# Rebalancing attention multiplies over steps 11 to 21, and loading two key blocks ahead of the rest

## The chip, the cores and the metric

One core of one Trainium2 chip. The metric is the device time of one execution in microseconds (us), as the median of several executions. Engines: PE does matrix multiplies and transposes, ACT the exponentials, DVE the copies, casts and small elementwise work, POOL issues most loads and prepares later keys, SP issues the first loads and the stores.

## The reference

Attention with queries pooled in pairs, then a feed-forward part that multiplies two projections.

```python
def _attn_ref(q, k, v):                       # (8, 8, 1152, 64) each
    q_pool = q.reshape(B, H, S // 2, 2, D).mean(axis=3)
    scores = np.matmul(q_pool, k.transpose(0, 1, 3, 2)) / np.sqrt(D)
    attn = np.exp(scores - np.max(scores, axis=-1, keepdims=True))
    attn = attn / (np.sum(attn, axis=-1, keepdims=True) + 1e-09)
    return np.matmul(attn, v)

def _moe_ref(x, w1, w2, w3, w_out):           # x: (4608, 512)
    return ((x @ w1) * (x @ w2) @ w3) @ w_out
```

## The kernel before

The 64 heads are worked on in 32 pairs. The scores of all pairs are one long row of 324 chunks; three chunks make a step, so there are 108 steps. In each step PE computes three chunks of scores into three buffers (`psc`), ACT turns each into exponentials in a ring (`er`), PE multiplies earlier exponentials with v (`attend`, so many per step as the list `PVS` says), and up to two side jobs run: one in a buffer of its own (kind F), one in one of the three score buffers (kind X). Side jobs are the transposes of the next pair's queries and keys, and feed-forward work. A tail of feed-forward work follows.

The first pair's keys and queries are loaded in pieces into the end of the ring:

```python
    q0f = spare(2304, FP32).rearrange("p (t d) -> p t d", d=D)
    k0a = spare(512, FP32).rearrange("p (u j d) -> p u j d", u=2, d=D)
    k0b = spare(1792, FP32).rearrange("p (u j d) -> p u j d", u=2, d=D)
    # ... cut ...
    def load_first():
        src = k[0, 0:2].rearrange("u (p j) d -> p u j d", j=NJ)
        qs = q[0, 0:2].rearrange("u (p t) d -> (u p) t d", t=18)
        nc.sync.dma_start(out=k0a, in_=src[:, :, 0:2, :])
        for c in parts:
            r = slice(2 * c.start, 2 * c.stop)
            nc.sync.dma_start(out=q0f[:, r], in_=qs[:, r])
        nc.sync.dma_start(out=k0b, in_=src[:, :, 2:NJ, :])
    # ... cut: prep_first; stage_keys casts key blocks, move_keys transposes them ...
        spin(25, 128)          # filler multiplies
        stage_keys(0)
        move_keys(0)
        spin(8, 128)
        queries(0)
        spin(5, 128)
        scores(0)
        expo(0)
        queries(1)
        spin(1)
        stage_keys(1)          # casts blocks 2 and 3
        def some():
            move_keys(1)
            stage_keys(2)      # casts blocks 4 to 8
            spin(1)
```

The loads of the pairs after the first are issued in a fixed order, on POOL:

```python
    load_v(0)
    load_q(1)
    load_k(1)
    load_w3(0, 1)
    load_w3(1, 1)
    load_wo(0)
    load_k(2)
    load_q(2)
    load_v(1)
    # ... cut ...
```

The list, and the part of a step that uses it:

```python
    PVS = [
        0, 9, 13, 18, 22, 28, 22, 23, 22, 23, 40, 22, 28, 22, 23, 22, 23, 45,
        45, 18, 18, 18, 18, 18, 45, 18, 27, 45, 45, 18, 18, 18, 26, 18, 27, 21,
        # ... cut ...
    ]
    for it in range(NIT):
        # ... cut: fetch side jobs ...
        for w in range(BURST):
            # ... cut: some(), rest(), the first side jobs ...
            if it or w:
                scores(BURST * it + w)
                expo(BURST * it + w)
        # ... cut: loads, prep_stage (pools queries and casts keys on DVE), prep_groups ...
        n = PVS[it]
        left = 45 - nb % 45
        brief = bool(queue) and queue[0][2] == 1
        a = left if left < n else 8 if brief and it > 8 and 8 < n < 40 and 8 < left < 45 else 0
        pv(a)
        if head():
            group("F")
        if head() and (n < 40 or urgent or it < 17):
            group("X")
        pv(n - a)
        # ... cut ...
```

The softmax here doesn't subtract the row's maximum and nothing guards it: scores larger than these inputs give would overflow.

Of the kernel before, what the change touches and what calls it, by code (L numbers as in the profile page):

```python
# [15 lines left out]
NJ = 9  # L16
# [7 lines left out]
def kernel(  # L24
# [11 lines left out]
    nc = tc.nc  # L36
# [88 lines left out]
    def new_kq(P):  # L125
        if P % 2 == 0:
            kTs[P // 2] = ab.tile([128, 2, NJ, 128], FP16, tag="kT", bufs=2, name="kT")
            qTs[P // 2] = ab.tile([128, NJ, 128], FP16, tag="qT", bufs=2, name="qT")
        o = 64 * (P % 2)
        kT[P] = kTs[P // 2][:, P % 2]  # L130
        qT[P] = qTs[P // 2][:, :, o:o + 64]

    def copy_v(P):
        nc.vector.tensor_copy(out=vts[P % 4][:, :, :, 0:D], in_=vst.pop(P))
# [39 lines left out]
    def spare(n, dt=FP16):  # L174
        nonlocal end
        end -= n
        return er[:, 1, end:end + n].bitcast(dt) if dt != FP16 else er[:, 1, end:end + n]
# [3 lines left out]
    k0b = spare(1792, FP32).rearrange("p (u j d) -> p u j d", u=2, d=D)  # L181
# [4 lines left out]
# [4 lines that stand above are left out]
        for c in parts:  # L190
            r = slice(2 * c.start, 2 * c.stop)
            nc.sync.dma_start(out=q0f[:, r], in_=qs[:, r])  # L192
        nc.sync.dma_start(out=k0b, in_=src[:, :, 2:NJ, :])

    def spin(n, w=512):
        t = psum.tile([128, 512], FP32, tag="ff", bufs=1, name="spin")
        for _ in range(n):
            nc.tensor.matmul(t[:, 0:w], ones[:, 0:128], ones[:, 0:w], start=True, stop=True)

    def prep_first():  # L200

        new_kq(0)
        kc = new_kc(0)
        src = q0f.rearrange("p (c two) d -> p c two d", two=2)
        js = (slice(0, 2), slice(2, 4), slice(4, NJ))

        def stage_keys(n):
            j = js[n]
            copy = nc.vector.tensor_copy if n else nc.scalar.copy
            copy(out=kc[:, j].rearrange("p j u d -> p u j d"),  # L210
                 in_=k0b[:, :, j.start - 2:j.stop - 2] if n else k0a)

        def move_keys(n):
            j = js[n]
            tag = "ff" if n == 2 else "po"
            if n:
                tk = psum.tile([128, 1024], FP16, tag=tag, bufs=1, name="tk")
                keys(0, tk, range(j.start, j.stop))
            else:
                tk = psum.tile([128, 512], FP32, tag=tag, bufs=1, name="tk")  # L220
                for i in range(2):
                    nc.tensor.matmul(tk[:, 128 * i:128 * i + 128],
                                     kc[:, i].rearrange("p u d -> p (u d)"), ident,
                                     start=True, stop=True)
            copy = nc.vector.tensor_copy if n else nc.scalar.copy
            copy(out=kT[0][:, j].rearrange("p j f -> p (j f)"),
                 in_=tk[:, 0:128 * (j.stop - j.start)])

        def queries(h):
            r = parts[h]  # L230
            nc.vector.tensor_tensor(out=q0p[:, r], in0=src[:, r, 0, :], in1=src[:, r, 1, :],
                                    op=ALU.add)
            dt, w = (FP16, 1024) if h else (FP32, 512)
            tq = psum.tile([128, 2, w], dt, tag="psc", bufs=3, name="tq")[:, 0]
            for c in range(r.start, r.stop):
                o = 64 * (c - r.start)
                for u in range(2):
                    x = slice(64 * u, 64 * u + 64)
                    if h:
                        nc.tensor.transpose(tq[x, o:o + 64], q0p[x, c], ident[x, x])  # L240
                    else:
                        nc.tensor.matmul(tq[x, o:o + 64], q0p[x, c], ident[x, x],
                                         start=True, stop=True)
            copy = nc.vector.tensor_copy if h else nc.scalar.copy
            copy(out=qT[0][:, r],
                 in_=tq[:, 0:64 * (r.stop - r.start)].rearrange("p (c f) -> p c f", f=64))

        spin(25, 128)
        stage_keys(0)
        move_keys(0)  # L250
        spin(8, 128)
        queries(0)
        spin(5, 128)
        scores(0)
        expo(0)
        queries(1)
        spin(1)
        stage_keys(1)

        def some():  # L260
            move_keys(1)
            stage_keys(2)
            spin(1)

        def rest():
            move_keys(2)
            copy_v(0)
            del kcs[0]

        return some, rest  # L270
# [168 lines left out]
    def ffn_groups(t):  # L439
# [79 lines left out]
        out=ident, in_=ident, compare_op=ALU.not_equal, fill=1.0,  # L519
# [46 lines left out]
    def head():  # L566
        while not queue and gens:
            g = next(gens[0], None)
            if g is None:
                gens.pop(0)  # L570
            else:
                queue.append(g)
        return bool(queue)
# [35 lines left out]
    for t, c, h in PLAN:  # L609
        early.append((t, w3_group(c) if h is None else T_group(c, h)))  # L610

    PVS = [
        0, 9, 13, 18, 22, 28, 22, 23, 22, 23, 40, 22, 28, 22, 23, 22, 23, 45,
        45, 18, 18, 18, 18, 18, 45, 18, 27, 45, 45, 18, 18, 18, 26, 18, 27, 21,
        34, 35, 18, 27, 18, 27, 25, 30, 45, 45, 18, 18, 18, 18, 18, 45, 18, 27,
        45, 45, 18, 18, 18, 26, 18, 27, 21, 34, 35, 18, 27, 18, 27, 25, 30, 45,
        45, 18, 18, 18, 18, 18, 45, 18, 27, 45, 45, 18, 18, 18, 26, 18, 27, 21,
        34, 35, 18, 27, 18, 27, 25, 30, 45, 45, 18, 18, 18, 18, 18, 45, 45, 18,
    ]
    reached = []  # L620
    next_unit = 0
    for it in range(NIT):
        at = it * BURST * CH / PAIR
        while early and it >= early[0][0]:
            queue.append(early.pop(0)[1])
        while next_unit < EARLY:
            last_b = (512 * (next_unit + 1) - 1) // SQ
            if it < 3 or reached[it - 2] < 360 * (last_b + 1):
                break
            gens.append(ffn_groups(next_unit))  # L630
            next_unit += 1
        for w in range(BURST):
            if it == 0 and w == 2:
                some()
            if it == 1 and w == 1:
                rest()
            if it == 2 and w == 2:
                queue[0:0] = prep_groups(1)
                prepped = 2
# [5 lines that stand above are left out]
        if 6 <= staged < NPE and it >= first_it(staged) - 3:  # L645
            prep_stage(staged)
            staged += 1
        while 8 <= loaded < NPE + 2 and at >= loaded - 3.4:
            load(loaded)
            loaded += 1  # L650
        urgent = False
        if prepped < NPE:
            if it >= first_it(prepped) - (1 if prepped < 5 else 2):
                queue[0:0] = prep_groups(prepped)
                prepped += 1
                urgent = True
        elif prepped < NP and at >= prepped - 1.95:
            prep_dma(prepped)
            if loaded < NP:
                settled(prepped)  # L660
                load_two(loaded)
                loaded += 2
            prepped += 2
        if NPE <= copied < NP and at >= copied - 1.1:
            copy_v(copied)
            copied += 1
# [4 lines that stand above are left out]
        assert nb + n <= NPV and ready(nb + n - 1, BURST * it)  # L671
        pv(a)
        if head():
            group("F")
        if head() and (n < 40 or urgent or it < 17):
            group("X")
        pv(n - a)
        if staged < 6 and it >= first_it(staged) - (2 if staged < 5 else 3):
            prep_stage(staged)
            staged += 1  # L680
            more_loads(staged)
        if copied < NPE and at >= copied + (0.25 if copied < 5 else 0):
            copy_v(copied)
            copied += 1
        reached.append(nb)
# [43 lines left out]
```

## Time and profile before

| | before |
|---|---|
| median, lowest, highest of 3 runs | 416.02, 416.01, 416.2 us |
| execution that was profiled | 416.7 us (span of the core 414.9) |
| PE busy | 406.0 us, 98% |
| ACT busy | 326.3 us, 79% |
| DVE busy | 198.8 us, 48% |

In a list of instructions in order of time, the first number is the start in us after the span's start, the second the duration of the group, then come engine, source line, operation, what is written and read, shapes, and how many instructions the group holds. The bracket gives the engine's idle time just before it, and what ended that.

DVE stands still for 0.80 us until the first pair's keys have landed, and casts blocks 2 and 3 at 7.72. The last line is the pooling of pair 2's queries; its load had landed at 20.44, so DVE did not wait for it.

### The profile page before, as it was taken

Reading aid. Unit: us, or ns where it says so; the run is one execution under the profiler, and the core shown is the slowest. Engines: PE = TensorE matmul, PEld = TensorE weight load, DVE = VectorE, ACT = ScalarE, POOL = GpSimd, SP = SyncE. Lnnn points to the kernel's source line nnn. Section 1 sums busy time; section 2 is a strip of 40 time slices with the busy share of each in tenths; the row PEclk is TensorE's granted clock in tenths of the full one; section 3 lists DMA queues with packets and bytes.
Section 4 is the critical chain, followed back from the end, with each engine's and each line's share of the span. In section 5 each row is a group of like instructions: output and inputs, shape, how many; then the busy total and the mean of one; then the engine's idle time right before and its main releaser. Section 6 shows DMA issues by size and latency. Waiting matters only on the chain.

```text
span 414.9 us, 12697 instructions
## 1 busy us (share of the span) xinstructions
PE 406.0 (98%) x5489; PEld 270.4 (65%) x5489; DVE 198.8 (48%) x407; ACT 326.3 (79%) x357; POOL 121.2 (29%) x161
## 2 busy tenths in 40 slices
PE   8999999999999999999999999999999999999996
PEld 5577787766775677666866686667665876644443
DVE  2546756455445553554455744554455434714141
ACT  5999989889888889988888899898888889133332
POOL 6442422343625163333334314361430000000000
PEclk9999999999999999999999999999999999999999
DMA  8999999799999999999799969997994350050402
GB/s 187 203 204 184 182 206 193 132 162 159 158 187 206 160 166 195 197 160 160 139 211 156 169 93 204 175 170 110 182 174 89 44 90 20 14 117 2 101 0 103
DMA packets 96249, 59.76 MB, mean 144 GB/s; under 512 B 65472, under 2 KB 86464, under 8 KB 96192
## 3 DMA queue, kind: packets, MB, share of 16 engines
q0 software_dynamic: 26928, 32.97, 50.9%
q1 hardware_dynamic: 69264, 25.97, 36.4%
q8 instruction: 43, 0.70, 0.7%
q14 instruction: 14, 0.11, 0.1%
HBM read 67.11 MB, written 9.44 MB: 184 GB/s over the span
## 4 chain that ended last, share of the span: by engine, by line
PE 90%; ACT 6%; DMA 1%; issue 1%; SPq 0%; DVE 0%; ACTq 0%
PE po L354 20%; PE psc L321 19%; PE pa L448 16%; PE pp L471 16%; PE pb L448 15%; ACT er L340 6%; PE pT L432 3%; DMA er<-in_k_dram 1%; PE w3t L420 1%; PE t L169 0%; SPq L192 0%; SPq L189 0%; DVE osb L483 0%; DVE kc L210 0%; PE tk L169 0%
## 5 line engine op out<-in xcount | busy, mean ns | idle before, releaser
L340 ACT ACTIVATE er<-psc 128x1024 f16<-128x1024 f32 x325 | 307.6, 1025 | 40.8 <-PE psc L321 40.7
L354 PEld LDWEIGHTS <-er 128*128 128x128 f16 x2880 | 103.3, 97 | 22.2 <-issue 6.3
L354 PE MATMUL po<-vt,er 128*128 128x65 f16 x2880 | 110.4, 193 | 0.0
L321 PE MATMUL psc<-qT,kT 64*128 64x256 f16 (+7 forms) x1154 | 95.2, 285 | 3.0 <-ACT er L340 2.5
L465 DVE TENSOR_TENSOR gT<-pb,asb 128x512 f16<-128x512 f32 x72 | 50.1, 696 | 55.8 <-PE pb L448 55.1
L448 PE MATMUL pa<-xT,w1sb 128*128 128x512 f16 x288 | 74.2, 380 | 0.0
L448 PE MATMUL pb<-xT,w2sb 128*128 128x512 f16 x288 | 74.1, 380 | 0.0
L471 PE MATMUL pp<-T,gT 128*128 128x256 f16 (+1 forms) x488 | 67.9, 292 | 0.0
L321 PEld LDWEIGHTS <-kT 64*128 64x128 f16 x1154 | 45.5, 94 | 27.8 <-issue 8.8
L471 PEld LDWEIGHTS <-gT 128*128 128x128 f16 x488 | 45.7, 98 | 18.5 <-issue 3.7
L458 DVE COPY asb<-pa 128x512 f32<-128x512 f32 x56 | 38.7, 691 | 39.5 <-PE pa L448 38.5
L448 PEld LDWEIGHTS <-w2sb 128*128 128x128 f16 x288 | 26.4, 98 | 32.7 <-issue 3.9
L448 PEld LDWEIGHTS <-w1sb 128*128 128x128 f16 x288 | 25.0, 98 | 30.1 <-issue 6.2
L121 POOL TENSOR_TENSOR qp<-qst 128x1152 f16<-128x1152 f16 x12 | 28.3, 2355 | 51.7 <-issue 28.6
L483 DVE TENSOR_SCALAR osb<-pp 128x256 f32<-128x256 f32 x49 | 20.8, 425 | 38.6 <-PE pp L471 38.6
L367 DVE RECIPROCAL rz<-po 128x5 f32<-128x5 f32 x64 | 12.4, 193 | 47.3 <-PE po L354 46.9
L141 POOL COPY kc<-kst 128x576 int32<-128x576 int32 x24 | 16.3, 679 | 57.7 <-issue 43.5
L371 DVE TENSOR_TENSOR xn<-po,rz 128x320 f16<-128x320 f32 x64 | 31.5, 492 | 2.2
L95 POOL DMA_DIRECT2D vst<-in_v_dram x32 | 23.4, 742 | 11.5 <-DVE kc L165 2.7
L480 ACT ACTIVATE osb<-pp 128x512 f32<-128x512 f32 (+1 forms) x12 | 7.0, 579 | 24.0 <-PE pp L471 21.8
L88 POOL DMA_DIRECT2D kst<-in_k_dram x31 | 22.7, 747 | 10.5 <-DVE rz L367 3.3
L456 ACT COPY asb<-pa 128x512 f32<-128x512 f32 x16 | 9.4, 585 | 16.5 <-PE pa L448 16.5
(49 smaller groups left out, 150.4 us busy)
## 6 DMA issues: line engine op xcount, KB each, us to landing
vst<-in_v_dram POOLq DMA_DIRECT2D x32, 288.0 KB, 10.2
qst<-in_q_dram POOLq DMA_DIRECT2D x31, 288.0 KB, 6.9
kst<-in_k_dram POOLq DMA_DIRECT2D x31, 288.0 KB, 12.2
out_dram<-osb SPq DMA_DIRECT2D x66, 128.0 KB, 2.9
w3h<-in_moe_w_dram POOLq DMA_DIRECT2D x3, 512.0 KB, 16.4
xT<-in_moe_w_out_dram POOLq DMA_DIRECT2D x4, 256.0 KB, 10.4
w1sb<-in_moe_w_dram POOLq DMA_DIRECT2D x2, 512.0 KB, 16.2
w2sb<-in_moe_w_dram POOLq DMA_DIRECT2D x2, 512.0 KB, 16.7
```

The costliest lines, as they stand in the source:

```text
L88: nc.gpsimd.dma_start(out=kst[P].rearrange("p u j d -> p u (j d)"), in_=k[b, h0:h0 + 2].rearrange("u (p j) d -> p u (j d)", j=NJ))
L95: nc.gpsimd.dma_start(out=vst[P].rearrange("p u j d -> p u (j d)"), in_=v[b, h0:h0 + 2].rearrange("u (p j) d -> p u (j d)", j=NJ))
L121: eng.tensor_tensor(out=qps[pp][r].rearrange("p c u d -> p u c d"), in0=src[:, :, :, 0, :], in1=src[:, :, :, 1, :], op=ALU.add)
L321: nc.tensor.matmul(t[:, u, o:o + ln].rearrange("p (c f) -> p c f", f=64), kT[P][x, j, :], qT[P][x, f0 // 64:(f0 + ln) // 64], start=True, ...
L340: nc.scalar.activation(out=o, in_=i, func=AF.Exp, bias=0.0, scale=SCALE)
L354: nc.tensor.matmul(po[P, u][:, VW * x:VW * x + D + 1], er[:, u, r:r + 128], vts[P % 4][:, u, j, 0:D + 1], start=(m == 0), stop=(m == 44), ...
L371: nc.vector.tensor_tensor(out=xn[:, P % 2, :, u, :], in0=acc[:, :, 0:D], in1=rz.to_broadcast([128, 5, D]), op=ALU.mult)
L448: nc.tensor.matmul(p, w[:, mc, ft * 128:ft * 128 + 128], xT[:, mc, t0:t0 + 512], start=(mc == 0), stop=(mc == NC - 1))
L458: nc.vector.tensor_copy(out=asb[ft], in_=p)
L465: nc.vector.tensor_mul(out=o, in0=p, in1=a)
L471: nc.tensor.matmul(p[:, 0:n], gT[:, ft, 128 * i:128 * i + 128], T16[:, ft, n * s:n * s + n], start=(ft == 0), stop=(ft == NF - 1))
L483: nc.vector.tensor_scalar_mul(out=osb, in0=p[:, 0:n], scalar1=1.0 / (SCL * SCL))
```

## The change: intent and diff

The intent: let the start of the kernel go on as soon as two more key blocks are there, instead of all seven; and give the steps with key preparation (12, 14, 19 to 21) more attention multiplies, taken from the heavy steps 11, 13, 17 and 18, so that PE and ACT wait for each other less. Totals agree again after step 21. The explicit list `SINGLE` names the steps that the old rule chose, so the side jobs stay where they were.

```diff
-        nc.sync.dma_start(out=k0b, in_=src[:, :, 2:NJ, :])
+        nc.sync.dma_start(out=k0b[:, :, 0:2], in_=src[:, :, 2:4, :])
+        nc.sync.dma_start(out=k0b[:, :, 2:7], in_=src[:, :, 4:NJ, :])
@@
-        spin(5, 128)
+        spin(4, 128)
         scores(0)
@@ PVS (the rest of the list is the same, in other line breaks)
-        0, 9, 13, 18, 22, 28, 22, 23, 22, 23, 40, 22, 28, 22, 23, 22, 23, 45,
-        45, 18, 18, 18, 18, 18, 45, [cut]
+        0, 9, 13, 18, 22, 28, 22, 23, 22, 23, 40, 12, 38, 12, 33, 22, 23, 35, 38,
+        20, 20, 31, 18, 18, 45, [cut]
@@
+    SINGLE = (17, 24, 27, 28, 44, 45, [cut])
@@
-        if head() and (n < 40 or urgent or it < 17):
+        if head() and it not in SINGLE:
             group("X")
```

## The prediction

> **What bounds the kernel now.** I read the page's busy table and its chain of waits first, then the engines' busy time in stretches of 5 us, to see where TensorE (PE) is idle at all.
>
> ```profile
> PE 406.0 (98%) x5489; PEld 270.4 (65%) x5489; DVE 198.8 (48%) x407; ACT 326.3 (79%) x357; POOL 121.2 (29%) x161
> PE 90%; ACT 6%; DMA 1%; issue 1%; SPq 0%; DVE 0%; ACTq 0%
> ...
> 5.00:10.00 5.00, 4.18 (x49) 2.04 (x44) 1.82 (x5) 3.34 (x5) 4.09 (x7) 1.00 1.06 204
> 70.00:75.00 5.00, 4.75 (x71) 3.72 (x71) 2.57 (x7) 5.00 (x6) 0.00 (x0) 1.00 1.18 207
> 75.00:80.00 5.00, 5.00 (x73) 3.36 (x72) 2.13 (x5) 3.97 (x5) 0.63 (x1) 1.00 0.96 170
> ```
>
> After length and colon the columns are PE, weight loads, DVE, ACT, POOL, granted clock, DMA share, GB/s. From 75 us until 411 us PE is busy in practically every stretch; all its idle time, about 5 us, lies before 75 us, apart from 3.7 us after its last multiply. PE's work is the same in both kernels but for one filler multiply. So the change can gain only what it takes out of PE's gaps before 75 us, and that passes one to one to the end unless something later stops PE.
>
> What makes those gaps I take from the instructions in order of time. ACT (the exponentials), then PE:
>
> ```profile
> 6.33 2.17 ACT L340 ACTIVATE er<-psc 128x1024 f16<-128x1024 f32 x3 [0.75 <-PE psc L321]
> 9.14 12.09 ACT L340 ACTIVATE er<-psc 128x1024 f16<-128x1024 f32 x13 [0.65 <-PE psc L321]
> ...
> 42.04 5.60 ACT L340 ACTIVATE er<-psc 128x1024 f16<-128x1024 f32 x6 [0.42 <-PE psc L321]
> 48.08 5.61 ACT L340 ACTIVATE er<-psc 128x1024 f16<-128x1024 f32 x6 [0.44 <-PE psc L321]
> ```
>
> ```profile
> 44.94 0.61 PE L321 MATMUL psc<-qT,kT 64*128 64x256 f16 x8 [0.29 <-ACT er L340]
> ...
> 48.69 0.43 PE L280 MATMUL t<-ident,qp 64*128 64x64 f16 x9
> 49.06 0.70 PE L169 MATMUL t<-ident,kc 128*128 128x128 f16 x9
> ...
> 50.98 0.61 PE L321 MATMUL psc<-qT,kT 64*128 64x64 f16 x8 [0.45 <-ACT er L340]
> ...
> 61.61 0.61 PE L169 MATMUL t<-ident,kc 128*128 128x128 f16 x8 [0.32 <-ACT er L340]
> ...
> 65.09 1.03 PE L432 MATMUL pT<-xT,w3T 128*128 128x256 f16 x8 [0.19 <-ACT er L340]
> ...
> 70.00 0.61 PE L321 MATMUL psc<-qT,kT 64*128 64x64 f16 x8 [0.18 <-ACT er L340]
> ...
> 72.83 0.61 PE L321 MATMUL psc<-qT,kT 64*128 64x256 f16 x8 [0.25 <-ACT er L340]
> ```
>
> From 9 to 38 us ACT never rests longer than 0.16 us. In steps 11 to 22 (38 to 75 us) it takes turns with PE: ACT waits 0.2 to 0.6 us at the start of a heavy step for scores, and PE waits in or after a light step for a score buffer that ACT has not emptied. There are three such buffers, and one is also lent to the second side job of a step. The steps with key preparation (12, 14, 18, 21) are light for PE. The six gaps shown sum to 0.29 + 0.45 + 0.32 + 0.19 + 0.18 + 0.25 = 1.68 us.
>
> **What the Trainium skill says.** "Perfetto Trace Analysis", section "Optimization Strategy": where regimes change over time, interleave them, and look at the gaps on the bounding engine. The trace fits: the gaps of both engines alternate. "DMA: Bandwidth & Descriptors", section "Issuing engines are not separate DMA queues": transfers from all issuing engines run on the same 16 DMA engines and interleave. It agrees: while transposes of the result run at 30 to 33 us, the loads write 0.41 MB in 3 us instead of about 0.60. Same page, "Specifications": 512 B is the smallest transfer at line rate. The new small load has runs of 2 x 64 x 4 = 512 B, just there; the first key load has that form, and landed 2.2 us after its issue. "TensorE: Matmul & The Clock Gate", "Back-to-back issue gap": columns / 1.2 ns when cold. The early fillers of 128 columns start 106.7 ns apart, as it says, and the clock is granted in full from 6.08 us.
>
> **The change part by part.**
>
> First keys. The load of key blocks 2 to 8 (448 KB, issued at 2.23, landed at 7.70 us) is split into blocks 2 and 3 (128 KB), then the rest; both stay behind the queries, which landed at 5.41. In proportion of bytes the small one lands at 5.41 + 2.29 x 128/448 = 6.1 us. DVE, which cast those keys at 7.72 when they landed, is free at 6.92 us (its query copy runs 6.60 to 6.92), so it can cast 0.80 us earlier. The next scores ended 1.38 us after the start of this cast (9.10), hence now at 8.30, before ACT is done with the second chunk (8.49). ACT's gap of 0.65 us at 9.14 closes: 0.65 us gained there. The remaining keys are cast after the first copy (about 8.0 us) and have landed by then.
>
> One filler less is 0.107 us of PE, but the scores behind it began at 5.75 and waited for ACT's copy that ended at 5.58, long after the weights were loaded: 0 to 0.03 us.
>
> Attention multiplies. The new list moves 10 from step 11 to 12, 10 from 13 to 14, and 17 from steps 17 and 18 to 19, 20 and 21 (2, 2, 13); the totals agree again after step 21. One costs about 0.031 us (45 in 1.4 us). Step 18 now puts 10 of them, and step 21 22 instead of 9, before the side jobs. The groups of side jobs keep their steps: the list of single-job steps names those that the old rule chose. I stepped PE and ACT by hand from step 11 to 23 with the durations above (exponential 0.915 us from start to start, 0.05 us from its end to the freed buffer). The gaps at 44.94 and 50.98 shrink to about 0.1 each, but a new one of 0.1 to 0.3 appears in the lightened steps 14 and 16. The one at 61.61 is filled by the 10 multiplies ahead of it; small ones of 0.1 to 0.3 stay in steps 18 to 22. If nothing but PE and ACT counted, 1.2 us would be gained by 72.83, beside the 0.65.
>
> **The rival that I think takes the first part back: loaded data.** The loads keep the DMA engines full up to 79 us: the trace's landings show each load of k, q or v landing 10 to 17 us after its issue, each issue waiting for an earlier landing. What arrives then does not come sooner because PE is ahead.
>
> ```profile
> 47.63 0.76 DVE L121 TENSOR_TENSOR qp<-qst 64x1152 f16<-64x1152 f16 x1 [0.18 <-DMA qst<-in_q_dram]
> 48.41 0.46 DVE L165 COPY kc<-kst 128x1152 f16<-128x1152 f16 x1
> ...
> 79.37 2.36 POOL L121 TENSOR_TENSOR qp<-qst 128x1152 f16<-128x1152 f16 x1 [10.50 <-PE psc L321]
> ```
>
> The first is the pooling of pair 5's queries: their load landed at 47.60, and DVE was waiting. Pooled at 48.39 and its keys at 48.87, they are transposed by PE at 48.69 and 49.06: slack 0.3 and 0.2 us. With 0.65 from the start and 0.6 from steps 11 to 14, PE would be there near 47.6. So it waits until about 48.45, and the keys until 48.93: only 0.13 of the lead is left. Ten more multiplies follow (+0.31), so the scores of step 15 start at 50.33 (before 50.15), and their second chunk, no longer held by ACT, at 50.58 (before 50.98). Stepping on from there: step 16's second chunk waits for ACT until 53.75 (0.1 ahead of before), step 19 about 0.2 ahead at equal multiplies done, step 20 0.6, step 21 0.8, and the second chunk of step 22 at 71.86 against 72.83: 0.97 us. This does not depend on the start.
>
> The second line names PE, but its load (queries of pair 9) landed at 79.20. From it follow 2.36 us of pooling, key copies and transposing DMAs; pair 8's queries landed at 87.38 and PE used them at 88.66. So whatever is gained, at most 1.25 us pass this point: a second limit.
>
> I take 0.15 us off the 0.97, for 256 more descriptors early and result transposes that now start sooner among the loads. That leaves 0.82: 416.02 - 0.82 = 415.2 us.
>
> **Rivals by their outcome.**
> 1. Data at pair 5 holds: gain 0.6 to 1.0, 415.0 to 415.4. For it: DVE already waits there. Against: landing times vary.
> 2. Pair 5 lands earlier, or the start's lead survives: capped by pair 8 at 1.25, 414.8. Against: the full DMA row.
> 3. Both data limits give way: 0.65 + 1.2 = 1.85, 414.2. I see no way for both.
> 4. The loads come later (smaller pieces, colliding transposes) and the lightened steps make new gaps: 0 to 0.4, 415.6 to 416.0. For it: my stepping left new gaps of 0.1 to 0.3 in steps 14, 16, 18, 19 and 20.
> 5. One filler less delays the granted clock by a window: some tenths at the start, which rival 1 swallows anyway.
>
> **Range and chances.** Rivals 1 and 2 have about 75%, 4 about 17%, 3 the rest. Range 414.6 to 415.8. 2% is 8.3 us, more than all PE idle time before 75 us together: 98% for within 2%.
>
> **What would show it.** The first keys' cast on DVE at 6.9 instead of 7.7 and ACT's gap at 9.14 gone (right for the start). Pair 5's pooling still starts at 47.5 to 47.9 us, now with DVE idle near 0.9 us for the query load, and a new PE gap of 0.5 to 1 us before the query transposes of step 14 (right for rival 1; if PE passes there before 48.2 us, I am wrong). PE's gaps at 61.61, 65.09 and 70.00 mostly gone; step 23's scores at 74.8 to 75.1 instead of 75.78; step 27's at 87.7 to 88.0, without a wait for the transposed queries (with one, rival 2 or 3). No PE gap after it.

## More of the kernel before

DVE in the first 24 us, in order of time:

```profile
7.72 0.31 DVE L210 CAST kc<-er 128x256 f16<-128x256 f32 x1 [0.80 <-DMA er<-in_k_dram]
...
20.88 0.74 DVE L121 TENSOR_TENSOR qp<-qst 64x1152 f16<-64x1152 f16 x1
```

## The result, and the profile after

| | before, same rounds | changed |
|---|---|---|
| median (lowest, highest), 4 runs each | 416.01 (415.94, 416.2) us | 416.76 (416.5, 417.21) us |
| ratio, 95% interval | | 1.0018 (1.0001 to 1.0036) |

A ratio is the mean time of one kernel's runs over the mean of the other's runs of the same rounds, so not quite the ratio of the medians. The class is "same", as predicted; but 415.2 us was predicted and 415.8 was the top of the range, so the predicted gain did not come. Whether the 0.75 us of loss in this first comparison is real is taken up below; repeated with more runs it was not there.

The busy table and the chain of waits of the changed kernel:

```profile
PE 406.6 (98%) x5488; PEld 270.0 (65%) x5488; DVE 198.4 (48%) x407; ACT 326.4 (79%) x357; POOL 120.9 (29%) x161
PE 90%; ACT 7%; issue 2%; DVE 0%; ACTq 0%
```

One filler fewer, otherwise the same work, and PE still bounds. So the time went into PE's gaps, and where can be read by comparing PE's clock positions: the start of each chunk's first score multiply in the changed kernel, minus that in the kernel before. It is -0.70 us at chunk 2 (the start's gain), still -0.70 at chunk 15, then -0.06 at chunk 18 (step 6), -0.27 at chunk 69 (step 23), -0.30 at chunk 225 (step 75), and -0.02 from chunk 231 to the end. So there are three places to explain: something takes 0.64 us in step 5, the list brings only 0.21 us by step 23, and 0.28 us is lost near 250 us, where nothing was changed.

**The start.** ACT, then DVE, of the changed kernel in the first 24 us:

```profile
6.23 14.30 ACT L341 ACTIVATE er<-psc 128x1024 f16<-128x1024 f32 x16 [0.71 <-PE psc L322]
```

```profile
6.74 0.59 DVE L211 CAST kc<-er 128x256 f16<-128x256 f32 x1
...
21.04 0.75 DVE L121 TENSOR_TENSOR qp<-qst 64x1152 f16<-64x1152 f16 x1 [0.78 <-DMA qst<-in_q_dram]
```

The cast of key blocks 2 and 3 starts at 6.74 and no longer waits for a load; ACT runs sixteen exponentials without a gap from 6.23 (before, it stopped for 0.65 us at 9.14). That is the predicted mechanism and, at 0.70, nearly the predicted size of 0.65. The third line is where the gain goes: pair 2's queries landed at 21.02 and DVE waited 0.78 us for them. PE around it, changed kernel, then before:

```profile
20.25 0.94 PE L322 MATMUL psc<-qT,kT 64*128 64x384 f16 x10
21.85 0.43 PE L281 MATMUL t<-ident,qp 64*128 64x64 f16 x9 [0.66 <-DVE qp L121]
...
41.25 0.39 PE L322 MATMUL psc<-qT,kT 64*128 64x512 f16 x2
41.90 0.61 PE L322 MATMUL psc<-qT,kT 64*128 64x64 f16 x8 [0.26 <-ACT er L341]
...
46.25 1.03 PE L433 MATMUL pT<-xT,w3T 128*128 128x256 f16 x8 [0.19 <-ACT er L341]
...
249.34 1.12 PE L322 MATMUL psc<-qT,kT 64*128 64x192 f16 x12
```

```profile
20.95 0.94 PE L321 MATMUL psc<-qT,kT 64*128 64x384 f16 x10
21.71 0.42 PE L280 MATMUL t<-ident,qp 64*128 64x64 f16 x9
...
249.64 0.85 PE L321 MATMUL psc<-qT,kT 64*128 64x192 f16 x12
```

PE came 0.70 us early to the scores (20.25) and waited 0.66 us for the pooled queries: the lead is gone at 21.85. It is a loaded-data limit, as predicted, but of pair 2 in step 5, not of pair 5 in step 14. At pair 5 nothing waited: its queries had landed at 46.87, and DVE, then PE, took them without a gap in front:

```profile
47.78 0.75 DVE L121 TENSOR_TENSOR qp<-qst 64x1152 f16<-64x1152 f16 x1
...
48.97 0.43 PE L281 MATMUL t<-ident,qp 64*128 64x64 f16 x9
```

**Late starts of ACT.** The last PE line shows the loss near 250 us: the same twelve score multiplies take 1.12 instead of 0.85 us, because PE is held inside the group by a score buffer that ACT has not emptied. ACT there and in step 11, before, then changed:

```profile
38.76 2.85 ACT L340 ACTIVATE er<-psc 128x1024 f16<-128x1024 f32 x3 [0.55 <-PE psc L321]
...
246.97 2.85 ACT L340 ACTIVATE er<-psc 128x1024 f16<-128x1024 f32 x3 [0.33 <-PE psc L321]
```

```profile
39.00 3.77 ACT L341 ACTIVATE er<-psc 128x1024 f16<-128x1024 f32 x4 [0.84 <-PE psc L322]
...
246.95 2.85 ACT L341 ACTIVATE er<-psc 128x1024 f16<-128x1024 f32 x3 [0.60 <-PE psc L322]
```

PE began the scores of chunk 225 at 246.48 before and at 246.18 in the changed kernel, 0.30 us earlier; yet the exponential starts at almost the same time. The bracket still blames PE, since that was the last event seen. The records of ACT's instructions one by one, numbered from 0, show that the wait itself had ended:

| ACT record number | before: what, start | changed: what, start |
|---|---|---|
| 445 | wait instruction, 246.91 | exponential before, 245.32 |
| 446 | exponential of chunk 225, 246.97 | wait instruction, 246.61 |
| 447 | wait instruction, 247.29 | exponential of chunk 225, 246.95 |
| 448 | wait instruction, 247.37 | wait instruction, 246.97 |

From the wait to the exponential it takes 0.06 us before and 0.34 us in the changed kernel. In both kernels record 447 is the one that comes late: before, it is a wait instruction that starts 0.32 us after the exponential's start, where 0.16 is usual, and the exponential runs meanwhile, so it costs nothing. In the changed kernel ACT's program is one instruction longer from early on (710 records instead of 709, of which 350 waits instead of 349), and record 447 is the exponential. The same is true of chunk 33 in step 11, with record 63 (38.64 to 39.00). 447 - 63 = 384 = 3 x 128. The extra instruction comes from the split load: the ring area of the first keys is overwritten by the exponential of chunk 9, which now has to wait for two loads instead of one.

That this is the cause had to be tested. "Runtime: NRT & Kernel Launch" in the Trainium skill, section "Instruction fetch mechanics", says that an engine's instructions are streamed in blocks of 256 (16 KiB) and that crossing a block is mostly hidden. Fetching would fit late instructions at fixed numbers; the profile page of both kernels counts two queues of kind "instruction", one with packets of about 16 KB (43 for 0.70 MB), one of about 8 KB (14 for 0.11 MB, so 128 instructions each if one has 64 bytes as the 256 in 16 KiB imply). The single packets in the trace tie the second queue to these engines: in the first trace of before, some of its packets start at 107.63, 178.91 and 317.16 us, when 193, 324 and 576 of ACT's records have started, and others at 47.46, 143.15 and 344.98, when 63, 191 and 448 of DVE's have, so near every 128th record after the 63rd. Most of ACT's start after the late record, so that record cannot wait for them; what exactly comes late no run here shows.

### The profile page after: what moved, and what is told of

The parts are those of the page before. It is cut to its first block, busy times and chain, and to the rows that moved or that the text cites. A ratio compares the mean times of both kernels' runs of the same rounds, so it can differ in the third digit from the quotient of the medians. Undisturbed runs are those within 1.5% of the kernel's fastest.

```text
span 414.8 us, 12698 instructions
## 1 busy us (share of the span) xinstructions
PE 406.6 (98%) x5488; PEld 270.0 (65%) x5488; DVE 198.4 (48%) x407; ACT 326.4 (79%) x357; POOL 120.9 (29%) x161
## 4 chain that ended last, share of the span: by engine, by line
PE 90%; ACT 7%; issue 2%; DVE 0%; ACTq 0%
PE po L355 20%; PE psc L322 19%; PE pa L449 16%; PE pb L449 15%; PE pp L472 15%; ACT er L341 7%; PE pT L433 2%; PE spin L199 1%; PE t L169 1%; PE w3t L421 1%; PE t L281 0%; DVE kc L165 0%; DVE kc L211 0%; DVE osb L484 0%; PE tq L243 0%
## 5 line engine op out<-in xcount | busy, mean ns | idle before, releaser
L88 POOL DMA_DIRECT2D kst<-in_k_dram x31 | 22.7, 746 | 11.1 <-DVE xn L372 5.1
```

Of the source, the lines that this page charges most:

```text
L88: nc.gpsimd.dma_start(out=kst[P].rearrange("p u j d -> p u (j d)"), in_=k[b, h0:h0 + 2].rearrange("u (p j) d -> p u (j d)", j=NJ))
```

## The experiments

Four calls, each with the kernel before on the same chip. Only e8's interval excludes 1; so what a part does is read from the traces, one execution each. The table gives PE's position against the first trace of before (us; minus is earlier) at the start of the scores of a chunk, from each run's own trace; "end" is the end of PE's last multiply. Chunks 2 and 15 belong to steps 0 and 5, 18 to 6, 33 to 11, 51 to 17, 69 to 23, 225 to 75, 231 to 77. In the first trace of before these times are 8.53, 20.95, 23.86, 38.27, 56.94, 75.78, 246.48, 252.81 and 411.27. That trace had a slow start (e15_null shows it), so a lead at chunk 2 is not by itself a gain; compare the columns within a row.

| run | 2 | 15 | 18 | 33 | 51 | 69 | 225 | 231 | end |
|---|---|---|---|---|---|---|---|---|---|
| changed kernel | -0.70 | -0.70 | -0.06 | -0.06 | +0.27 | -0.27 | -0.30 | -0.02 | -0.02 |
| e5_after | -1.16 | -0.09 | +0.22 | +0.23 | +0.55 | +0.01 | 0.00 | +0.27 | +0.28 |
| e1_null | +0.39 | +0.72 | +0.72 | +0.72 | +0.72 | +0.71 | +0.70 | +0.70 | +0.71 |
| e15_null | -0.57 | -0.57 | -0.57 | -0.57 | -0.57 | -0.57 | -0.59 | -0.59 | -0.59 |
| e2_split | -1.13 | -0.84 | -0.84 | -0.84 | -0.77 | -0.78 | -0.79 | -0.51 | -0.17 |
| e14_split | -1.26 | -0.93 | +0.08 | +0.08 | +0.15 | +0.14 | +0.13 | +0.42 | +0.42 |
| e4_spin | -0.68 | -0.68 | +0.01 | +0.01 | +0.01 | +0.01 | 0.00 | 0.00 | 0.00 |
| e3_pv | 0.00 | 0.00 | 0.00 | 0.00 | +0.03 | -0.50 | -0.51 | -0.51 | -0.51 |
| e9_pv_late | -0.76 | -0.76 | -0.76 | -0.76 | -0.76 | -1.30 | +1.32 | +1.32 | +2.34 |
| e10_pv_early | -0.61 | -0.62 | -0.62 | -0.62 | -0.59 | -0.59 | -0.61 | -0.61 | -0.61 |
| e6_before_act | -0.51 | -0.51 | -0.51 | -0.51 | -0.44 | -0.44 | -0.44 | -0.17 | -0.15 |
| e7_after_act | -0.38 | -0.38 | +0.53 | +0.53 | +0.55 | +0.01 | +0.01 | +0.01 | +0.03 |
| e8_after_act_q | -0.72 | -0.72 | -0.72 | -0.72 | -0.69 | -1.23 | -1.23 | -1.24 | -1.21 |
| e12_best | -0.71 | -0.71 | -0.71 | -0.71 | -0.68 | -1.22 | -1.22 | -1.22 | -1.20 |
| e11_pv_q | -0.53 | -0.53 | -0.53 | -0.53 | -0.49 | -1.04 | -1.05 | -1.05 | -1.05 |
| e13_split4 | -0.61 | +1.50 | +1.50 | +1.50 | +1.50 | +1.50 | +1.73 | +1.72 | +1.73 |
| e16_split4 | -1.20 | +4.34 | +4.34 | +4.34 | +4.34 | +4.34 | +4.58 | +4.57 | +4.57 |

The theory that stood after the result: the list gains less than predicted, the lead of the start is lost to the loads, and one wait more on ACT makes two exponentials late. The rivals: the split load itself delays the later loads; the whole difference is scatter between executions; the list makes new gaps of its own.

### First call: the parts of the change alone, 5 rounds

**e1_null** is the kernel before, unchanged, to learn what two equal kernels differ by.

> The kernel before once more, unchanged, as the floor of noise and for a second trace of it. All theories: ratio 1.000 within 0.0005. Its trace tells how far the landings of the loads and the PE gaps before 75 us move between executions: if the span is 414.2 and not 414.9, the trace that the prediction was read from was of a slow execution, and the comparison of the two first traces hides a loss of about 0.6 us. If exponential 33 or 225 starts 0.3 us late here too, those late starts are chance.

Measured: 416.88 us (416.36 to 417.39) against 416.75 (415.99 to 417.39, 9 runs) of before; ratio 1.0008 (0.9995 to 1.002). So executions of one kernel spread over 1.4 us here. In its trace PE was 0.72 us late by chunk 15: the trace records the full clock only from 10.19 us, in the first trace of before from 6.08. The median of this one kernel was 416.01 in the first comparison and is 416.75 here, so medians of a few runs on different occasions differ by over half a microsecond without a cause in the kernel.

**e2_split**: only the split load.

```diff
-        nc.sync.dma_start(out=k0b, in_=src[:, :, 2:NJ, :])
+        nc.sync.dma_start(out=k0b[:, :, 0:2], in_=src[:, :, 2:4, :])
+        nc.sync.dma_start(out=k0b[:, :, 2:7], in_=src[:, :, 4:NJ, :])
```

> Only the first-key load split. Theory A (loads land later because of the split): the chunk-2 scores start 0.7 us sooner, the queries of pair 2 land near 21.0 instead of 20.4 us, PE waits 0.5 to 0.7 us for their pooling in step 5, and the time is equal to before or up to 0.5 us longer. Theory B (the moved multiplies cost the time, the split is harmless): lead of 0.1 to 0.7 us after step 5, time 0.1 to 0.6 us shorter.

Measured: 416.45 us (416.39 to 417.17), ratio 1.0001 (0.9988 to 1.0013). PE led by 1.13 us at chunk 2 and kept 0.84, but lost 0.28 between chunks 225 and 231, just as the changed kernel did. So the list has no part in that loss. Between chunk 231 and the end another 0.34 was lost (its DVE and PE lines in order of time):

```profile
277.87 1.80 DVE L134 COPY vt<-vst 128x1152 f16<-128x1152 f16 x1
...
281.75 0.39 PE L322 MATMUL psc<-qT,kT 64*128 64x512 f16 x2 [0.25 <-DVE gT L466]
```

A copy that mostly takes 0.45 us took 1.80 while POOL was pooling queries (277 to 279.3 us), and PE waited for DVE. The long copy is no peculiarity of this trace: over all 18 traces this copy started 33 times while POOL was pooling, and in 32 of them it ended 0.32 to 0.33 us after the pooling did. Only here and in e9 did PE lose time near the end by it.

**e3_pv**: only the new list, with `SINGLE`.

```diff
-        [cut] 23, 40, 22, 28, 22, 23, 22, 23, 45, 45, 18, 18, 18, [cut]
+        [cut] 23, 40, 12, 38, 12, 33, 22, 23, 35, 38, 20, 20, 31, [cut]
-        if head() and (n < 40 or urgent or it < 17):
+        if head() and it not in SINGLE:
```

> Only the moved attention multiplies. Theory A: 0.2 to 1.0 us shorter than before (the hand-stepped 1.2 less new gaps). Theory B: 0.3 to 0.8 us longer than before. Theory C (a late start of the exponential of chunks 33 and 225, of 0.3 us each, belongs to the changed order of the program): about 0.5 us of gain is missing here and both late starts are in the trace.

Measured: 415.97 us (415.51 to 416.45), ratio 0.9986 (0.9972 to 1.0). PE is level with before until step 11, 0.50 us ahead at step 23, and keeps 0.51 to the end. The list works, with half of the predicted gain, and neither the loss at step 5 nor that at 250 us. What it trades in steps 11 to 16, before first (PE in order of time), then this run:

```profile
41.55 0.82 PE L321 MATMUL psc<-qT,kT 64*128 64x512 f16 x10
...
47.58 0.83 PE L321 MATMUL psc<-qT,kT 64*128 64x384 f16 x10
...
53.63 0.83 PE L321 MATMUL psc<-qT,kT 64*128 64x192 f16 x12
```

```profile
41.24 1.04 PE L321 MATMUL psc<-qT,kT 64*128 64x512 f16 x10
...
46.02 1.03 PE L432 MATMUL pT<-xT,w3T 128*128 128x256 f16 x8 [0.19 <-ACT er L340]
...
47.35 1.11 PE L321 MATMUL psc<-qT,kT 64*128 64x384 f16 x10
...
53.39 1.10 PE L321 MATMUL psc<-qT,kT 64*128 64x192 f16 x12
```

Each of the three groups of scores starts 0.23 to 0.31 us earlier, because fewer multiplies stand ahead of it, and lasts 0.22, 0.28 and 0.27 longer: PE comes before ACT has freed the buffer and is held inside the group. The line at 46.02 starts 0.81 after the eight transposes ahead of it, where 0.46 is what they take: 0.35 more. Together 1.12 us. What they replace are the two interrupted groups of before that the prediction shows by their second parts, at 44.94 and 50.98. Begun at 44.26 and 50.15, they took 1.29 and 1.44 us, where the undisturbed ones of twelve and ten multiplies above took 0.83 and 0.82: 0.46 + 0.62 = 1.08. So the waits were exchanged, not removed; chunk 51 starts 0.03 later than before.

**e4_spin**: only the filler.

```diff
-        spin(5, 128)
+        spin(4, 128)
         scores(0)
```

> Only one filler multiply less. All theories: within 0.1 us of before; the first scores start 0 to 0.1 us sooner. If it costs the clock a window, the granted clock comes after 6.1 us and the time is 0.2 to 0.6 us longer.

Measured: 416.69 us (416.1 to 417.56), ratio 1.0003 (0.9988 to 1.0017): nothing. In its trace the unsplit keys landed at 7.01 instead of 7.70, so PE led by 0.68 at chunk 2 without any split. And at step 5 it lost all of it, to pair 2's queries that landed at 21.09 (PE idle 0.71 us before their transposes at 21.92). So a lead can be lost there without a split load, and the first trace of before had the latest landing of the first keys of all nine traces with that load (6.89 to 7.70): the gain of the split is nearer 0.5 than 0.65. Over the seven traces with the split in two, the first three chunks' scores took 2.03 us from the first to the third start in the mean, over the nine without it 2.55.

### Second call: the instruction count of ACT, 5 rounds

**e5_after**: the changed kernel again, without an edit.

> The changed kernel once more, on the chip of the three below. If the late exponentials (theory C: one more wait instruction on ACT, from the split load's second semaphore, moves the program so that something every 128 instructions falls on the first exponential of step 11 and of step 75) are its loss: late by 0.28 to 0.30 us at chunks 33 and 225 again, PE loses 0.27 us at chunk 229 again, and the time is within 0.4 us of before. If they are chance, they are elsewhere or absent.

Measured: 416.51 us (416.16 to 418.15) against 416.41 (415.74 to 417.77, 11 runs) of before; ratio 1.0005 (0.9988 to 1.0023). The loss of the first comparison is not repeated. In its trace the lead of 1.16 us was lost at two loads: pair 1's keys (landed at 12.82) took 1.07, pair 2's queries the rest (PE idle 0.33 us). The list brought 0.22, and the loss at 250 us is 0.27, both as in the first trace of the changed kernel.

**e6_before_act**: the kernel before with one tiny copy of one element early on ACT. This makes ACT's program one instruction longer and changes nothing else.

```diff
+    seen2 = const.tile([1, 1], FP16)
@@
+        nc.scalar.copy(out=seen2, in_=ones[0:1, 0:1])
```

> The kernel before with one tiny copy added at the start of ACT, while ACT waits for the first keys, so that its later program stands one instruction further on; nothing else. Theory C: the exponentials of chunks 33 and 225 now start about 0.28 us late here too, as in the changed kernel, PE loses about 0.27 us after chunk 225, and the time is 0.3 to 0.4 us longer than before. Rival (the late starts come from the transfers of the split load): no late start, time equal to before.

Measured: 416.89 us (416.53 to 418.35), ratio 1.0014 (0.9997 to 1.003). Its ACT in the two windows:

```profile
38.55 2.86 ACT L342 ACTIVATE er<-psc 128x1024 f16<-128x1024 f32 x3 [0.84 <-PE psc L323]
...
246.80 2.86 ACT L342 ACTIVATE er<-psc 128x1024 f16<-128x1024 f32 x3 [0.60 <-PE psc L323]
```

0.84 and 0.60: the waits of the changed kernel, to the hundredth, without the changed kernel's loads or list. PE loses 0.27 between chunks 225 and 231. At step 11 only 0.07 is lost, because the old list leaves PE work to do there.

**e7_after_act**: the changed kernel with the same copy, so two instructions longer than before.

```diff
+    seen2 = const.tile([1, 1], FP16)
@@
+        nc.scalar.copy(out=seen2, in_=ones[0:1, 0:1])
```

> The changed kernel with the same tiny copy on ACT, so that its program stands two instructions further on than before's. Theory C: no late start at chunks 33 and 225; the moved multiplies then give about 0.5 us in steps 11 to 22, as they did alone (against 0.21 in the changed kernel's trace), no loss at chunk 229; 0.4 to 0.6 us shorter than the changed kernel. Rival: the late starts stay, time equal to the changed kernel's.

Measured: 415.79 us (415.29 to 417.66), ratio 0.9988 (0.9968 to 1.0008). ACT in the same windows:

```profile
39.28 2.86 ACT L343 ACTIVATE er<-psc 128x1024 f16<-128x1024 f32 x3 [0.55 <-PE psc L324]
...
246.98 2.85 ACT L343 ACTIVATE er<-psc 128x1024 f16<-128x1024 f32 x3 [0.32 <-PE psc L324]
```

0.55 and 0.32 again, as in before. Adding an instruction took the two late starts away: the list now brings 0.52 us between chunks 33 and 69 (0.21 and 0.22 in the two traces of the changed kernel), and nothing is lost at chunk 225. One instruction more makes it late and two do not: this supports the position of the instruction as the cause, and rules out the load, the list, and longer work as such. All 18 traces agree: the five with 710 records on ACT (changed kernel, e2, e5, e6, e14) have both late starts, 0.34 to 0.35 us after the wait, and the thirteen with 709 or 711 have neither. What the trace of this run lost is the start: pair 2's queries landed at 21.61, and PE was idle for 0.92 us.

**e8_after_act_q**: the same, and pair 2's queries loaded before its keys.

```diff
     load_wo(0)
-    load_k(2)
     load_q(2)
+    load_k(2)
     load_v(1)
```

> As the one above, and the queries of pair 2 loaded ahead of its keys instead of behind them. Theory A (the lead of 0.7 us from the first keys is lost where PE waits in step 5 for the pooling of those queries, which land at 20 to 21 us): they land 1.2 us sooner, near 19.3 us, the keys near 20.6; PE's wait in step 5 falls from up to 0.7 to 0.2 us or less and the lead at chunk 18 is 0.5 to 0.7 us; 0 to 0.5 us shorter than the one above. Rival: the lead was lost to chance in the landings, and the time is the same.

Measured: 415.46 us (415.41 to 416.3), ratio 0.998 (0.9965 to 0.9995). Pair 2's queries landed at 19.31. Its PE in step 5:

```profile
20.99 0.42 PE L283 MATMUL t<-ident,qp 64*128 64x64 f16 x9
```

The transposes of those queries start at 20.99 (21.71 before) without a wait in front of them; the lead of 0.72 is kept, the list adds 0.51, and PE ends 1.21 us earlier than in the first trace of before.

### Third call: the halves of the list (3 rounds), and the better version (5 rounds)

**e9_pv_late**: the old list in steps 11 to 14, the new one in 17 to 21; `SINGLE` as in e3, here and in e10 and e11.

```diff
-        [cut] 40, 22, 28, 22, 23, 22, 23, 45, 45, 18, 18, 18, [cut]
+        [cut] 40, 22, 28, 22, 23, 22, 23, 35, 38, 20, 20, 31, [cut]
```

> Of the moved multiplies only those of steps 17 to 21; steps 11 to 14 as before. If the whole 0.50 us of the list comes from here (in the trace of the list alone, PE was level with before at the scores of step 17, at equal multiplies done): PE is 0.45 to 0.55 us ahead of before between the scores of step 11 and those of step 23. If both halves give: 0.2 to 0.3 us.

Measured: 416.63 us (416.09 to 419.02) against 416.49 (415.94 to 417.38, 11 runs) of before; ratio 1.0012 (0.9988 to 1.0037). In the trace the lead grows by 0.54 us from chunk 51 to 69. PE there, in order of time:

```profile
60.68 0.68 PE L169 MATMUL t<-ident,kc 128*128 128x128 f16 x9
...
63.90 1.04 PE L432 MATMUL pT<-xT,w3T 128*128 128x256 f16 x8
...
65.56 0.61 PE L321 MATMUL psc<-qT,kT 64*128 64x448 f16 x6 [0.21 <-ACT er L340]
```

The waits of before at 61.61 (0.32) and 65.09 (0.19) are gone, the first because the ten multiplies of step 18 stand ahead of the transposes; one of 0.21 remains there, and one of 0.20 at 71.54. The profiled execution was the slowest of the batch, 419.02 us. PE stopped once for 2.50 us at 152.6 us, which the profile puts down to "issue"; no other trace has this. A late fetch would fit, but is not tested: the 17th of the 16 KB instruction packets starts at 152.42, when 4545 records of PE and its weight loads have started, against 4281 to 4467 in the other traces. PE also waited 0.40 us twice near 283 us for DVE, whose copy of v took 2.49 us while POOL pooled, as in e2. These take the time of this one execution out of the comparison, not the reading at 75 us.

**e10_pv_early**: the reverse.

```diff
-        [cut] 40, 22, 28, 22, 23, 22, 23, 45, 45, 18, 18, 18, [cut]
+        [cut] 40, 12, 38, 12, 33, 22, 23, 45, 45, 18, 18, 18, [cut]
```

> Only the moves of steps 11 to 14. If they only exchange one wait for ACT against another: 0.0 us within 0.05 between the scores of step 11 and of step 23, new waits for ACT near 46.0, 47.8 and 53.9 us in place of those at 44.9 and 51.0. The prediction's stepping gave them 0.1 to 0.4 us.

Measured: 416.9 us (416.16 to 417.76), ratio 1.0008 (0.9991 to 1.0026). From chunk 33 to 51 PE loses 0.03, and gains nothing later. So in these traces the moves in steps 11 to 14 are worth nothing, and the whole 0.5 us of the list comes from steps 17 to 21.

**e11_pv_q**: the list, and pair 2's queries before its keys; no split, no copy on ACT.

```diff
     load_wo(0)
-    load_k(2)
     load_q(2)
+    load_k(2)
@@
-        [cut] 40, 22, 28, 22, 23, 22, 23, 45, 45, 18, 18, 18, [cut]
+        [cut] 40, 12, 38, 12, 33, 22, 23, 35, 38, 20, 20, 31, [cut]
```

> The kernel before with all the moved multiplies and the queries of pair 2 loaded ahead of its keys; no split of the first keys, no filler taken away, no copy on ACT. About 0.5 us ahead at chunk 69 and no late start; 0.5 to 0.7 us shorter than before. If the split is worth its 0.7 us at the start once the queries of pair 2 come in time, this is 0.2 to 0.7 us longer than the run below.

Measured: 415.81 us (415.62 to 417.01), ratio 0.9991 (0.9975 to 1.0007). In the trace the queries landed at 19.21, PE kept 0.53 through step 5, and ended 1.05 us early. With the whole load of the first keys and without any change in ACT's count it ends within 0.15 us of the next one, and the medians of the two are 0.07 us apart: once the queries come in time, a worth of the split is not shown.

**e12_best** is e8_after_act_q again.

> Once more the changed kernel with the tiny copy on ACT and the queries of pair 2 ahead of its keys, to see whether it beats before on another chip or at another time: 0.6 to 1.2 us shorter than before, a lead of 0.5 to 0.8 us at chunk 18 in its trace and 1.0 to 1.3 us at chunk 69. If its trace was a lucky one, the lead at chunk 18 is 0 or less.

Measured: 415.88 us (415.36 to 417.08), ratio 0.9988 (0.9971 to 1.0005). The trace repeats the first one within 0.01 to 0.02 us at every chunk of the table. Both timings are below before, by 0.20 and 0.12 per cent, one with an interval that excludes 1. Its traces end earliest of all; by times it is not separated from e3, e7 and e11 (0.9986, 0.9988 and 0.9991).

### Fourth call: do smaller pieces delay the later loads? Single looks

The question left from e2 to e8: in five traces with the split and the old order, pair 2's queries landed at 20.19 to 21.61 (mean 21.06), in eight without the split at 20.03 to 21.09 (mean 20.44). If the additional small pieces cause this, four pieces should make it worse.

**e13_split4** and **e16_split4**: the load in four pieces of two blocks.

```diff
-        nc.sync.dma_start(out=k0b, in_=src[:, :, 2:NJ, :])
+        for j in (2, 4, 6, 8):
+            w = min(2, NJ - j)
+            nc.sync.dma_start(out=k0b[:, :, j - 2:j - 2 + w], in_=src[:, :, j:j + w, :])
```

> The kernel before with the first-key load in four pieces (2, 2, 2 and 1 blocks) instead of two. Theory A (smaller pieces make every later load land later): the queries of pair 2 land later still than in the split kernels so far (20.2 to 21.6 us, mean 21.0), at 21.5 us or more, and PE waits in step 5. Rival (chance in the landings): 20.0 to 21.1 us as in the unsplit kernels.

> The four pieces once more, as the first of this call. Theory A: 21.5 us or more. Rival: 20.0 to 21.1 us.

**e14_split** is e2_split, **e15_null** the kernel before, for comparison.

> The split alone, a second trace. Theory A: queries of pair 2 at 20.7 to 21.6 us. Rival: 20.0 to 21.1 us. The late starts at chunks 33 and 225 are there in any case (theory C).

> The kernel before, a third trace. Both: queries of pair 2 at 20.0 to 21.1 us; key blocks 2 to 8 land at 6.9 to 7.7 us; no late start at chunks 33 and 225.

Measured: 418.25 us (e13), 421.08 (e16), 417.06 (e14), 416.12 (e15), before 416.12; single executions, so of unknown state. Pair 2's queries landed at 20.99 and 21.41 with four pieces, and at 21.16 in e14_split, no later than with two. So this test did not support the theory: a delay of about 0.6 us goes with the split in these traces, the ranges overlap, and doubling the pieces did not enlarge it. One link can be read, though. In every trace with the old order this load was issued 0.29 to 0.30 us after pair 0's v had landed, and v landed at 9.06 us in the mean of nine traces with the whole load, at 9.37 with two pieces (seven), at 10.33 and 10.51 with four. Whether that delay reaches the landing of the queries stays open. What four pieces did was something else, shown by PE in e13, then e16:

```profile
11.18 0.45 PE L169 MATMUL tk<-ident,kc 128*128 128x128 f16 x5 [2.04 <-DVE kc L212]
```

```profile
11.86 0.72 PE L169 MATMUL tk<-ident,kc 128*128 128x128 f16 x5 [3.31 <-DVE kc L212]
```

The last piece (block 8) landed at 10.50 and 11.18 us, after pair 0's whole v, which POOL had issued; PE had been ready for it at 9.14 and 8.55. PE waited 2.04 and 3.31 us, and in e16 the granted clock then fell to half from 11.1 to 17.9 us. e14_split lost its lead of 0.93 at pair 2's queries (PE idle 1.02 us before 21.99) and 0.29 at chunk 225: of five split traces with the old load order, only e2 passed step 5 without a loss.

The four-piece traces also repeat the effect of the instruction count, on another engine. ACT has 711 records there, by two more waits and without the tiny copy, and no late start at chunks 33 and 225. DVE has 515 instead of 514, because one cast now waits for three loads, and DVE's record 191 = 63 + 128 starts 0.42 and 0.43 us after its wait, where the same instruction of before took 0.13. Before, then e13:

```profile
141.46 0.69 DVE L465 TENSOR_TENSOR gT<-pb,asb 128x512 f16<-128x512 f32 x1 [0.17 <-PE pb L448]
```

```profile
143.24 0.69 DVE L467 TENSOR_TENSOR gT<-pb,asb 128x512 f16<-128x512 f32 x1 [0.46 <-PE pb L450]
```

PE loses 0.23 us at chunk 131, which waits for a buffer that DVE empties; in the table this is the step between chunks 69 and 225 of both rows, and no other kernel has it.

e15_null, with 416.12 us the same as before, was 0.57 us ahead of the first trace of before at every chunk: the trace from which the prediction was worked out came from a slow start.

## Why the prediction was wrong, point by point

- **PE bounds, and only gaps before 75 us can change: half right.** PE bounds. But a gap appeared at 250 us, where "no PE gap" was predicted.
- **First keys, 0.65 us: right in mechanism, a little large.** The cast, ACT's closed gap and the -0.70 us came as told. Other traces show about 0.5, as the load of the first trace had landed latest.
- **One filler less, 0 to 0.03 us: right** as far as times can show (e4: ratio 1.0003).
- **Rival 1, loaded data takes the start back: right in kind, wrong in place.** The prediction looked for the tightest slack and found pair 5 in step 14 (0.3 us). PE never waited for pair 5, and the PE gap of 0.5 to 1 us in step 14 did not come: e8 started those transposes at 48.02, without a wait and before the 48.2 that the prediction had named as its sign of being wrong; the queries of pair 5 had landed at 46.84 there, not 47.60. (The 10 to 17 us from issue to landing were misread too: that very load took 18.7, from 28.91 to 47.60, and the first ones 6 to 7; and 48.69 less the two leads is 47.44, not 47.6.) The load that took the lead was pair 2's queries in step 5, in four of the five split traces with the old order, and in e5 also pair 1's keys. The landing times of one load scatter by a microsecond between executions, more than the slack that was read from a single trace.
- **Attention multiplies, 0.97 us by step 22: the step that failed first.** Alone they gave 0.51 (e3), in the changed kernel 0.21. The prediction had PE 0.6 us early at the query transposes of step 14, half of it ten multiplies put off; in e3 they start at 48.74, 0.05 later than before. The hand-stepping missed that three groups of scores would be held inside by ACT, for 0.22 to 0.28 us each, because PE now arrives earlier; it allowed new gaps of 0.1 to 0.3 in steps 14 and 16, but in steps 11 to 16 the waits only changed places. Steps 11 to 14 are worth nothing (e10), steps 17 to 21 0.54 (e9).
- **Rival 4, new gaps and later loads, given about 17%: the nearest to what happened.** The lightened steps did make new waits; that the loads come later because of smaller pieces is not shown.
- **What was not in it at all: the added wait on ACT.** It cost 0.30 us in the lightened step 11 (0.51 against 0.21 between chunks 33 and 69) and 0.28 at chunk 225. The same engine order with one wait instruction more was taken for no change. e6 made the loss with one idle instruction, e7 removed it with another.
- **The sum as the runs show it:** list -0.51, late start in step 11 +0.30, at chunk 225 +0.28: +0.07 us. The start's -0.5 to -0.7 was lost to loads in four of the five split traces with the old order. That is the time of before, within the scatter, and so it was measured in the second comparison (1.0005); that gain and losses cancel so nearly is chance. The predicted gain of 0.82 rested on the list alone, since the prediction had itself given up the start's share.
- **Range: too narrow, from too few runs.** Three executions within 0.2 us suggested a precision that the kernel does not have: its 31 later executions in the first three calls spread from 415.74 to 417.77, with medians of 416.75, 416.41 and 416.49. The first comparison's 1.0018 rests on four runs of before, 415.94 to 416.2, at the fast end of that spread, and is not shown to be an effect of the change.

What stays open: what exactly ACT's late instruction waits for; whether the split delays the landing of pair 2's queries; the 2.50 us stop in e9.

## What to carry to other kernels

Where an engine issues hundreds of instructions, look at whether a change adds or removes even one wait on it, and after the change compare the same instruction's idle time far from the change: a start that is 0.28 us late at fixed instruction numbers could be moved off the critical exponential by one tiny instruction, and DVE showed the same at its record 191 when it had one wait more. Before a lead at the start is counted as gain, go through every load that is used soon after it, in order of use, with the landing times of several executions; with the load that is needed first put ahead in the queue (pair 2's queries), all three traces (e8, e11, e12) kept the lead of the start through step 5, where four of five with the split and the old order lost it. And estimate the scatter from runs of the kernel on different occasions before predicting tenths of a per cent.

## What the Trainium skill lacked or had wrong

- "Runtime: NRT & Kernel Launch", section "Instruction fetch mechanics": it says that the cost of crossing a block of 256 instructions is mostly hidden. If the late starts are fetches, which no run here shows, they are not hidden where they hit an engine that others wait for: ACT's records 63 and 447, 3 x 128 apart, came 0.28 us late where they were exponentials (0.16 in the kernel before, where they were waits), and cost PE 0.27 to 0.29 us each time that such a record was chunk 225's exponential. The page has neither that distance nor a cost in time; its blocks of 16 KiB fit PE's packets here (43 of 16 KB for 10991 records), while ACT's and DVE's packets are of 8 KB.
- No page has it: equal loads at equal places of the order land up to 1.06 us apart between executions (pair 2's queries, 20.03 to 21.09 us in eight traces), which is more than the slacks of 0.2 to 0.3 us on which a schedule like this one is balanced.
- "TensorE: Matmul & The Clock Gate", section "What you observe": it puts the change to the full clock at about 4 us, give or take 0.5, for back-to-back multiplies. PE here is busy without a pause only until about 4.7 us, so the comparison is loose. Full clock was granted between 3.44 and 10.19 us after the span's start in the 18 traces, with fillers from 0.8 us on, and with the latest of these PE was 0.72 us behind the first trace.
